# Loads of the inverse transform three ahead instead of five, in place of an output tail cut into column halves

## The chip, the cores and the metric

The kernel runs on one core of one Trainium2 chip. The metric is the device time of one execution in microseconds (us). Engines are named as in the profile: PE is TensorE (PEld its weight loads), DVE VectorE, ACT ScalarE, POOL GpSimd, SP SyncE; SPq, ACTq and POOLq are the queues in which these engines issue DMA transfers.

## The reference

Two computations that share nothing but the output tensor, whose two column halves they fill.

Part A is a recurrent attention block. The 2048 rows of x are taken in 64 segments of 32. Each segment is set behind 8 memory rows; the 40 rows h are projected and attend to each other in 32 heads of 128; the first 8 rows of the result are the next segment's memory. So the segments run one after the other.

```python
mem = mem0
for s in range(64):
    h = concat([mem, x[32 * s:32 * s + 32]])            # 40 x 1024
    q, k, v = h @ Wq, h @ Wk, h @ Wv                    # each 40 x 4096 (32 heads x 128)
    p = softmax(where(mask, q @ k.T / sqrt(128), -1e9)) # mask: a memory row sees all, others no later row
    o = (p @ v) @ Wo                                    # 40 x 1024
    mem, out[s] = o[:8], o[8:]
```

Part B is a long convolution. A kernel K of 2048 taps for each of 1024 channels is the real part of a sum over 128 complex exponentials; y is the convolution of u with K by a transform of length 4096, taken back to time, and out = y + u * Dskip. Only the last step matters here: each piece of the inverse transform needs its piece of u again.

## The kernel before

**Part B runs first, and part A's weights are loaded under its end.** The inverse works through 32 chunks (`todo`, four column quarters of eight). `inverse` (L1316) multiplies on PE (L1313), scales on ACT (L1329), multiplies the chunk of u by Dskip (L1330) and adds (L1331) on DVE, and POOL sends the chunk out (L1332). `load_inverse` (L1270) fetches a chunk of u through SP (L1273) into one of six tiles `uu`. `inverses` (L1286) does one chunk and then issues the load of the chunk NIV - 1 = 4 places further on in what is left, so the loads run NIV = 5 chunks ahead of use. With six tiles, the load of chunk n + 5 takes the tile of chunk n - 1 and waits until that chunk has gone out. SP issues in program order: whatever stands behind such a load waits with it. Behind it stand part A's weights: the generator `residents` issues blocks of 512 KB (L229), a few at a time, from the loop over b and after each of the last eight chunks (ten after the first of them, L1388).

**Part A's loop (`part_a`, L373) goes over 64 segments.** A weight unit is 128 x 2048 bf16 (512 KB). A segment needs 64 units: 8 each for k, q and v in two halves of the heads, and 16 for the output projection (o). 49 stay in SBUF, 3 are held partly in PSUM banks ("kept": k 0 7, q 0 7, o 15) and are copied into SBUF each segment (L292), and 12 are streamed from HBM each segment by SP (L297) into four tiles `wst`, in the order of use; the load of a streamed unit takes the tile of the fourth one before it. `STREAM` and `STREAM_O` name the streamed ones. PE works through the units in order (L381 for q, k and v, L489 for o): the 32 rows are the stationary side, four column strips of PE run at once, and a whole unit takes 0.2165 us from start to start. Between them stand transposes (L392), scores (L406, L410) and value products (L460, L464).

**The seam of two segments.** The eight memory rows of the last projection must be transposed into `hT` (L369) before the next segment's first unit. In the kernel before, the last two output units (13 and 15) are run in column halves, first columns 0 to 127 into `pp`, then columns 128 to 255 into a bank of their own (`po`). ACT copies the first half out (L593) while the second runs; one transposition (`memory(0)`, L368, L369) serves the units of even kc; the other (`memory(1)`) stands after the next segment's first unit, in a part of the bank `pl` that also holds the last value product. The kept unit k 0 7 is copied partly by ACT (L327) and partly by DVE. ACT's copies of `pl` and `pp` into the output tile are L608 and L609. The copy of the second value product `o1` out of PSUM is made in two parts (L477), and the output units are taken in the order 8, 10, 12, 14, 9, 11, so that the first four need its first part alone.

Everything that lives only within a segment stands in one hand-placed block of SBUF (`arena`); `AT` holds the places.

Of the kernel before, what the change touches and what calls it, by code (L numbers as in the profile page):

```python
# [10 lines left out]
BF16 = mybir.dt.bfloat16  # L11
F32 = mybir.dt.float32
I32 = mybir.dt.int32
ALU = mybir.AluOpType
# [7 lines left out]

STREAM = {("k", 0): (2,), ("q", 0): (2,), ("k", 1): (1, 5), ("q", 1): (4,), ("v", 0): (2, 7), ("v", 1): (4, 7)}
STREAM_O = (4, 8, 13)

BANK = {("k", 0): "b0", ("q", 0): "b1", ("k", 1): "b2", ("q", 1): "b0", ("v", 0): "b3", ("v", 1): "b2"}
KEPT = {("k", 0, 7): (("K7a", 0, 512), ("K7b", 512, 512), ("K7c", 1024, 512), ("K7d", 1536, 384), (None, 1920, 128)),
# [3 lines left out]
SLOTS = 4  # L33

ARENA = 5984
AT = {"K7a": 3072, "K7b": 0, "K7c": 4864, "K7d": 4096, "ob": 2048, "pk": 1024, "vx": 4352, "Q7a": 3072, "Q7b": 4960,
      "k0": 0, "q0": 4352, "KT0": 3072, "QT0": 0, "k1": 3072, "q1": 0, "pn0": 2048, "pt0": 5344, "KT1": 3072, "QT1": 0,
      "pb0": 3072, "V0": 2048, "L0": 0, "o0": 3072, "V1": 0, "pn1": 5248, "pt1": 5664, "pb1": 1024, "lb1": 2048,
      "ln1": 2048, "lt1": 2368, "L1": 3072, "o1": 4960, "Oa": 1024, "Ob": 3584}


def weight_blocks(Wq, Wk, Wv, Wo):
# [190 lines left out]
def part_a(ctx, tc, x, src, WD, HE, seg_len, out_a, ahead, W_res, rest, places, first):  # L233
    nc = tc.nc
    S, Dm = x.shape
    M = 8
    SL = seg_len
    E = 128
    KC = Dm // 128
    NS = S // SL  # L240
    assert SL == 32 and M == 8 and Dm == 1024 and HE == 4096
    XM = 24
# [5 lines left out]
    ident, mask, BD, BDx, BDL, hT = ahead.consts  # L248
# [10 lines left out]
    between = {}  # L259

    def unit(key):
        if key in rest:

            rest.remove(key)
            load_resident(tc, wres, src, key, W_res, None, places.pop(0)() if places else None)
        if key in W_res:
            return W_res[key]
        if key in KEPT:
            return ahead_of.pop(key) + halves.get(key, [])
        between.pop(key, lambda: None)()  # L270
        if key in first:
            return first.pop(key)
        return stage(key, WD[key][:])
# [8 lines left out]
    def at(name, *dims):  # L282

        n = int(np.prod(dims))
        t_ = arena[:, AT[name] // 2:AT[name] // 2 + n]
        if len(dims) == 1:
            return t_
        names = "abc"[:len(dims)]
        return t_.rearrange("p (%s) -> p %s" % (" ".join(names), " ".join(names)), **dict(zip(names, dims)))

    def words(out, in_):
        nc.vector.tensor_scalar(out=out.bitcast(I32), in0=in_.bitcast(I32), scalar1=0, scalar2=None, op0=ALU.bitwise_or)  # L292
# [7 lines left out]
    def load_kept(key):  # L300
        t_ = first.pop(key) if key in first else stage(key, src(key))
        kept[key] = {}
        for n in (1,) if key in HALF else (0, 1):
            kept[key][n] = ps_k.tile([128, 512], F32, name="keep", tag="keep%d" % sum(len(b) for b in kept.values()))
            words(kept[key][n][:], t_[:, 1024 * n:1024 * n + 1024])
        if key in HALF:
            t_ = ahead.low["half"] if key[0] == "q" else wres.tile([128, 1024], BF16, name="Whalf")
            nc.sync.dma_start(out=t_[:], in_=src(key)[:, 0, :] if key[0] == "o" else src(key)[:, 0:1024])
            halves[key] = [(0, 1024, t_)]
# [6 lines left out]
            words(t_, kept[key][lo // 1024][:, lo % 1024 // 2:(lo % 1024 + n) // 2])  # L316
            ahead_of[key].append((lo, n, t_))

    def fetch_bits(eng, key, pieces):

        for name, lo, n in pieces:
            t_ = at(name, n) if name else S_[:, 0:n]
            bits = kept[key][lo // 1024][:, lo % 1024 // 2:(lo % 1024 + n) // 2]
            if eng is nc.vector:
                words(t_, bits)
            else:
                eng.copy(out=t_, in_=bits.bitcast(BF16))  # L327
            ahead_of[key].append((lo, n, t_))

    def columns(w, lo, n):  # L330

        if not isinstance(w, list):
            return [(0, w[:, lo:lo + n])]
        return [(max(lo, l_) - lo, t_[:, max(lo, l_) - l_:min(lo + n, l_ + n_) - l_]) for l_, n_, t_ in w if l_ < lo + n and lo < l_ + n_]
# [28 lines left out]
    load_kept(("k", 0, 7))  # L363
    fetch(("k", 0, 7))
    pk = load_pk(0)

    def memory(j):
        nc.tensor.transpose(out=tr_o[j].rearrange("p a b -> p (a b)"), in_=osb[:, 128 * j:128 * j + 128], identity=ident[:])  # L368
        nc.vector.tensor_copy(out=hT[:, :, XM:SL].rearrange("p (q j) r -> p j q r", j=2)[:, j], in_=tr_o[j][:, :, XM:SL])  # L369

    between["q", 0, 2] = lambda: load_kept(("q", 0, 7))
    between["v", 0, 7] = lambda: load_kept(("o", 15))
    for s in range(NS):  # L373
        def quads(m, t, kcs, a=None):
            if a is None:
                a = ps.tile([128, 512], F32, name="acc", tag=BANK[m, t])
            for kc in kcs:
                w = unit((m, t, kc))
                for g in range(4):
                    for o_, rhs in columns(w, 512 * g, 512):  # L380
                        nc.tensor.matmul(a[32 * g:32 * g + 32, o_:o_ + rhs.shape[1]], lhsT=hT[:, kc, :], rhs=rhs,  # L381
                                         start=(kc == 0), stop=(kc == KC - 1), tile_position=(0, 32 * g), skip_group_check=True)
            return a
# [87 lines left out]
            pv(p[:], t, V, pb.rearrange("p a b c -> p a (b c)"), lbs)  # L471
            return p

        def evac_o(p, name, parts=1):
            o, n = at(name, 4, 4, SL), 4 // parts
            for i in range(0, 4, n):
                nc.scalar.copy(out=o[:, i:i + n], in_=p[:, i:i + n, :].rearrange("p a (g q) -> p a g q", g=4))  # L477
            return o

        def pv_l(pl, t, V, L):  # L480

            pv(pl, t, V, L[:, 0].rearrange("p (a b) k -> p a (b k)", a=4), [L[:, 1].rearrange("p a k -> p (a k)")])

        def oblock(po, u, w, oT, lo, n, start=False):
            for hh in range(2):
                h = 2 * u + hh
                for qt in range(4):
                    for o_, rhs in columns(w, 1024 * hh + 256 * qt + lo, n):
                        nc.tensor.matmul(po[32 * qt:32 * qt + 32, o_:o_ + rhs.shape[1]], lhsT=oT[:, h % 4, (h % 16) // 4, :], rhs=rhs,  # L489
                                         start=start and hh == 0, stop=(h == 31), tile_position=(0, 32 * qt), skip_group_check=True)  # L490

        def oproj(po, us, oT):
            for u in us:
                oblock(po, u, unit(("o", u)), oT, 0, 256)

        a = quads("k", 0, (0,))
        if s:
            fetch_bits(nc.vector, ("k", 0, 7), KEPT["k", 0, 7][0:1])
            memory(1)
            fetch_bits(nc.vector, ("k", 0, 7), KEPT["k", 0, 7][1:2])  # L500
        quads("k", 0, (2, 4, 6, 1, 3, 5, 7), a)
        k0 = evac(a, "k0")
        a = quads("q", 0, range(0, 6))
        fetch(("q", 0, 7))
# [10 lines left out]
        vx = load_vx(s)  # L515
# [63 lines left out]
        powers(sc1, 1)  # L579
        oproj(pp[:, 1, :], range(0, 5), o0)  # L580
        pv1 = pv_x(1, V1, pb1, [lb1])
        o1 = evac_o(pv1, "o1", 2)
        lt1 = turn(weigh(sc1, 1, "ln1"), "lt1")
        oproj(pp[:, 1, :], range(5, 8), o0)
        L1 = left_blocks(lt1[:, 0:4, :], lt1[:, 4, :], "L1")
        fetch(("o", 15))
        oproj(pp[:, 1, :], (8, 10, 12, 14, 9, 11), o1)
        ob = at("ob", 2, 256)
        osb, base = ob[:, 0, :], ob[:, 1, :].bitcast(F32)
        ends = [(u, unit(("o", u))) for u in (13, 15)]  # L590
        for u, w in ends:
            oblock(pp[:, 1, 0:128], u, w, o1, 0, 128)
        nc.scalar.copy(out=osb[:, 0:128], in_=pp[:, 1, 0:128])  # L593
        nc.scalar.copy(out=base, in_=pp[:, 1, 128:256])
        rest_o = ps.tile([128, 128], F32, name="po", tag="b2")
        for u, w in ends:
            oblock(rest_o[:], u, w, o1, 128, 128, u == 13)
        last = ps.tile([128, 512], F32, name="pl", tag="b1")
        pv_l(last[:, 0:128].rearrange("p (a k) -> p a k", a=4), 1, V1, L1)
        if s + 1 < NS:  # L600
            tr_o = [ps.tile([128, 4, SL], BF16, name="tro", tag="b0")[:], last[:, 256:320].bitcast(BF16).rearrange("p (a b) -> p a b", a=4)]
            memory(0)
        nc.vector.tensor_tensor(out=osb[:, 128:256], in0=rest_o[:], in1=base, op=ALU.add)
        if s + 1 < NS:
            ahead_of["k", 0, 7] = []
            fetch_bits(nc.scalar, ("k", 0, 7), KEPT["k", 0, 7][2:])
            pk = load_pk(s + 1)
        nc.scalar.copy(out=ob[:, 1, 128:256], in_=last[:, 0:128])  # L608
        nc.scalar.copy(out=ob[:, 1, 0:128], in_=pp[:, 0, 0:128])  # L609
        if s + 1 < NS:  # L610
            stores(s, ob)

# [61 lines left out]
def part_b(ctx, tc, u, A_re, A_im, B_re, B_im, C_re, C_im, log_dt, Dskip, out_b, ahead, copies, residents, first_state):  # L674
# [37 lines left out]
    with tc.tile_pool(name="b_par", bufs=1) as par, tc.tile_pool(name="b_parh", bufs=2) as parh, tc.tile_pool(name="b_mg", bufs=2) as mg, \  # L712
# [54 lines left out]
        def columns(tm):  # L767
            return tm[:].rearrange("p c (k n) -> p c k n", k=4)
# [496 lines left out]
        for j, op in ((0, ALU.add), (1, ALU.subtract)):  # L1265
            v.tensor_tensor(out=Bt[:, kc, j], in0=Y[:, 0], in1=Y[:, 1], op=op)

    NIV = 5

    def load_inverse(dq, c):  # L1270
        r, mc = c // 4, c % 4
        uu = iv.tile([128, 2, DQ], BF16, name="uu", tag="uu", bufs=NIV + 1)
        sy.dma_start(out=uu[:], in_=u_v[r][:, mc:mc + 2, DQ * dq:DQ * dq + DQ])  # L1273
        return uu

# [272 lines left out]
```

## Time and profile before

| what | value |
|---|---|
| times of three runs | 2107.09, 2106.52, 2100.48 us; median 2106.52 |
| the profiled execution | 2107.09 us, its span 2105.4 us |
| busy share of the span | PE 90%, DVE 65%, PEld 57%, ACT 53%, POOL 18% |
| mean granted PE clock | 0.972 |
| first chunk of u loaded | 511.4 us |
| first PE work of part A | 701.56 us |
| first transposition of the memory (end of the first segment) | 759.99 us |
| last one (end of segment 63) | 2020.32 us |

From the last two rows, 62 segments lie between 759.99 and 2020.32 us, 20.33 us each; the shortest usual period is 19.90 us. A row of the timeline gives start, duration, engine, line, operation, output<-input, how many instructions were merged, and in brackets the idle time before and what ended it. A row of the waits gives who waited for whom, us in total, how often, and the longest.

### The profile page before, as it was taken

What the parts mean: (1) busy time and instruction counts of PE and PEld (TensorE: products, weight loads), DVE (VectorE), ACT (ScalarE), POOL (GpSimd) and SP (SyncE); (2) the same over time, 40 slices, a digit from 0 to 9 for tenths busy, and PEclk for the clock granted to TensorE, in tenths of its full rate; (3) what the DMA queues carried; (4) which work ended last, traced back from release to release, by engine and by line L of the source; (5) the groups of instructions that cost most, each with busy time, mean ns of one, the idle gap of its engine ahead of it and who ended that gap; (6) DMA issues with size and microseconds to landing.
All of it is one profiled execution on the core that took longest, in us unless ns stands there. A gap on an engine that the chain in (4) does not pass through costs nothing.

```text
span 2105.4 us, 81063 instructions
## 1 busy us (share of the span) xinstructions
PE 1886.3 (90%) x34694; PEld 1190.3 (57%) x34694; DVE 1368.4 (65%) x3227; ACT 1117.5 (53%) x2170; POOL 388.9 (18%) x780
## 2 busy tenths in 40 slices
PE   2799999978999779999999999999999999999989
PEld 1365665657788435555555555555555555555544
DVE  8689999889898236555565555655556565555650
ACT  5899999951323335445445454454545454454430
POOL 3133433452011101111111111111111111111120
PEclk8799999989999789999999999999999999999999
DMA  7696985665635899999999999999999899999991
GB/s 193 172 252 206 262 238 161 181 190 185 224 131 168 320 341 337 325 333 331 326 335 332 339 331 328 336 337 333 336 328 336 311 336 331 326 334 329 330 348 34
DMA packets 344029, 590.94 MB, mean 281 GB/s; under 512 B 108536, under 2 KB 220184, under 8 KB 341620
## 3 DMA queue, kind: packets, MB, share of 16 engines
q1 hardware_dynamic: 297016, 528.00, 74.3%
q0 software_dynamic: 10544, 33.69, 4.8%
q10 hardware_dynamic: 36108, 24.07, 3.7%
q8 instruction: 272, 4.46, 0.8%
q14 instruction: 89, 0.73, 0.1%
HBM read 530.86 MB, written 65.26 MB: 283 GB/s over the span
## 4 chain that ended last, share of the span: by engine, by line
PE 47%; DMA 19%; ACT 16%; DVE 9%; issue 7%; SPq 2%; POOL 1%; ACTq 0%; DVEq 0%; POOLq 0%
PE acc L381 22%; DMA wst<-WD_v 8%; PE pp L489 8%; DMA wst<-WD_o 6%; PE pe L638 3%; PE tr L392 2%; ACT sn L1142 2%; ACT nr L1151 2%; PE yp L1313 2%; ACT E L1125 2%; PE hps L1087 2%; ACT arena L327 2%; DMA arena<-PKd 1%; PE pa L1117 1%; PE pro L167 1%
## 5 line engine op out<-in xcount | busy, mean ns | idle before, releaser
L381 PEld LDWEIGHTS <-a_hT 128*32 128x32 bf16 x12352 | 339.0, 96 | 335.2 <-issue 82.4
L387 ACT CAST arena<-acc 128x512 bf16<-128x512 f32 x384 | 225.0, 586 | 339.1 <-PE acc L381 315.9
L381 PE MATMUL acc<-W,a_hT 128*32 128x512 bf16 x4864 | 377.2, 383 | 0.3 <-issue 0.3
L489 PEld LDWEIGHTS <-arena 128*32 128x32 bf16 x9216 | 216.1, 97 | 107.9 <-issue 58.4
L381 PE MATMUL acc<-wst,a_hT 128*32 128x512 bf16 x2304 | 233.3, 383 | 21.5 <-DMA wst<-WD_v 15.5
L292 DVE TENSOR_SCALAR arena<-keep 128x256 int32<-128x256 int32 (+1 forms) x386 | 143.4, 399 | 76.1 <-PE acc L381 72.6
L381 PE MATMUL acc<-MF,a_hT 128*32 128x512 bf16 x2048 | 171.3, 383 | 0.0
L489 PE MATMUL pp<-W_o,arena 128*32 128x256 bf16 x4608 | 163.0, 275 | 7.4 <-DMA W_o<-in_A_Wo_dram 7.4
L395 POOL COPY arena<-arena 128x128 bf16<-128x128 bf16 x128 | 37.6, 294 | 707.8 <-PE tr L392 373.9
L426 ACT ACTIVATE sc<-sc 128x160 f32<-128x160 f32 (+1 forms) x192 | 63.9, 333 | 160.9 <-DVE sc L423 157.6
L430 DVE TENSOR_REDUCE a_mx<-sc 128x4 f32<-128x160 f32 (+1 forms) x192 | 73.1, 381 | 87.3 <-ACT sc L426 87.3
L167 PE MATMUL pro<-xTl,wsl 128*128 128x512 bf16 x512 | 121.5, 389 | 8.4 <-ACT xTl L111 5.2
L1087 PEld LDWEIGHTS <-MF 128*128 128x128 bf16 x1024 | 102.2, 100 | 29.2 <-issue 8.6
L422 DVE TENSOR_REDUCE a_mx<-sc 128x4 f32<-128x160 f32 (+1 forms) x192 | 71.6, 373 | 68.6 <-PE sc L410 68.6
L513 DVE COPY arena<-tr 128x512 bf16<-128x512 bf16 x64 | 27.2, 425 | 126.3 <-PE tr L392 126.3
L453 POOL TENSOR_TENSOR arena<-arena,a_BD 128x128 bf16<-128x128 bf16 x128 | 51.6, 403 | 302.0 <-DVE arena L440 198.0
L1313 PE MATMUL yp<-Bt,MI 128*128 128x256 bf16 x680 | 105.5, 277 | 0.8 <-ACT yb L1329 0.8
L1087 PE MATMUL hps<-KT,MF 128*128 128x256 bf16 x720 | 93.3, 281 | 14.0 <-DVE x L1256 11.0
L477 ACT CAST arena<-pv 128x256 bf16<-128x256 f32 (+1 forms) x192 | 79.1, 449 | 47.0 <-PE pp L460 35.3
L1125 ACT ACTIVATE E<-pa 128x648 bf16<-128x648 f32 x128 | 91.4, 714 | 19.0 <-PE pa L1117 11.6
L167 PEld LDWEIGHTS <-wsl 128*128 128x128 bf16 x512 | 50.9, 99 | 73.6 <-issue 21.1
L445 DVE TENSOR_TENSOR arena<-arena,a_BDx 128x512 bf16<-128x512 bf16 x128 | 57.5, 450 | 49.6 <-PE sc L410 47.7
(323 smaller groups left out, 4108.8 us busy)
## 6 DMA issues: line engine op xcount, KB each, us to landing
wst<-WD_v SPq DMA_DIRECT2D x256, 512.0 KB
wst<-WD_k SPq DMA_DIRECT2D x192, 512.0 KB
wst<-WD_o SPq DMA_DIRECT2D x192, 512.0 KB
wst<-WD_q SPq DMA_DIRECT2D x128, 512.0 KB
Ud<-ux POOLq DMA_DIRECT2D x16, 1024.0 KB, 5.0
uq<-Ud SPq DMA_DIRECT2D x32, 512.0 KB
wsl<-in_A_Wk_dram SPq DMA_DIRECT2D x16, 512.0 KB
wsl<-in_A_Wv_dram SPq DMA_DIRECT2D x16, 512.0 KB
```

What stands on the lines that cost most here:

```text
L167: nc.tensor.matmul(a[:], lhsT=w[:, kc, 128 * j:128 * j + 128], rhs=xTl[:, kc, :, :].rearrange("p s k -> p (s k)"), start=(kc == 0), stop=( ...
L292: nc.vector.tensor_scalar(out=out.bitcast(I32), in0=in_.bitcast(I32), scalar1=0, scalar2=None, op0=ALU.bitwise_or)
L381: nc.tensor.matmul(a[32 * g:32 * g + 32, o_:o_ + rhs.shape[1]], lhsT=hT[:, kc, :], rhs=rhs, start=(kc == 0), stop=(kc == KC - 1), tile_pos ...
L387: nc.scalar.copy(out=q, in_=a[:])
L422: nc.vector.tensor_reduce(out=m_, in_=x, axis=AX.X, op=ALU.max)
L426: nc.scalar.activation(out=flat(sc, i), in_=flat(sc, i), func=ACT.Exp, scale=scale)
L430: nc.vector.tensor_reduce(out=m_, in_=x, axis=AX.X, op=ALU.add)
L477: nc.scalar.copy(out=o[:, i:i + n], in_=p[:, i:i + n, :].rearrange("p a (g q) -> p a g q", g=4))
L489: nc.tensor.matmul(po[32 * qt:32 * qt + 32, o_:o_ + rhs.shape[1]], lhsT=oT[:, h % 4, (h % 16) // 4, :], rhs=rhs, start=start and hh == 0, ...
L1087: pe.matmul(s_[r][half][:, cs, :], lhsT=MF[:, kc, 4 * rr + mc, cs, :], rhs=rhs, start=(i == 0 and mc == 0), stop=(i == 1 and mc == 3), ski ...
L1125: sc.activation(out=T["E", r, e // 4][:, lo:lo + 8 * NE].rearrange("p (i c) -> p i c", i=2), in_=T.pop(("p", r, e))[:, :, 0:4 * NE], func= ...
L1313: pe.matmul(yp[:, b, :], lhsT=m_[:, b, cs, kc, :], rhs=Bt[:, kc, j, half, c_, :], start=(kc == 0 and cs == 0 and half == 0), stop=(kc == 3 ...
```

## The change

Two things. `NIV` becomes 3: the load of chunk n + 3 is issued after chunk n, into the same six tiles, so it takes the tile of chunk n - 3. And the seam of part A takes another form: all sixteen output units run whole, in order, into `pp`; then ACT copies both column halves, PE does the last value product into a bank of its own, both transposes and then goes on to the next segment, whose first eight units run without a break; DVE copies both memory parts and then all five pieces of the kept unit k 0 7. `o1` is copied in one piece. With this go another choice of the twelve streamed units, another place in the first segment where two kept units are loaded, and other places in the arena.

```diff
-STREAM = {("k", 0): (2,), ("q", 0): (2,), ("k", 1): (1, 5), ("q", 1): (4,), ("v", 0): (2, 7), ("v", 1): (4, 7)}
-STREAM_O = (4, 8, 13)
+STREAM = {("k", 0): (2, 3), ("q", 0): (4,), ("k", 1): (3,), ("q", 1): (4,), ("v", 0): (0, 6), ("v", 1): (1, 5)}
+STREAM_O = (1, 5, 9)
...
-    between["q", 0, 2] = lambda: load_kept(("q", 0, 7))
-    between["v", 0, 7] = lambda: load_kept(("o", 15))
+    between["q", 0, 4] = lambda: load_kept(("q", 0, 7))
+    between["v", 0, 6] = lambda: load_kept(("o", 15))
...
-        a = quads("k", 0, (0,))
-        if s:
-            fetch_bits(nc.vector, ("k", 0, 7), KEPT["k", 0, 7][0:1])
-            memory(1)
-            fetch_bits(nc.vector, ("k", 0, 7), KEPT["k", 0, 7][1:2])
-        quads("k", 0, (2, 4, 6, 1, 3, 5, 7), a)
+        a = quads("k", 0, (0, 2, 4, 6, 1, 3, 5, 7))
...
-        o1 = evac_o(pv1, "o1", 2)
+        o1 = evac_o(pv1, "o1")
...
-        oproj(pp[:, 1, :], (8, 10, 12, 14, 9, 11), o1)
+        oproj(pp[:, 1, :], range(8, 16), o1)
         ob = at("ob", 2, 256)
-        osb, base = ob[:, 0, :], ob[:, 1, :].bitcast(F32)
-        ends = [(u, unit(("o", u))) for u in (13, 15)]
-        for u, w in ends:
-            oblock(pp[:, 1, 0:128], u, w, o1, 0, 128)
-        nc.scalar.copy(out=osb[:, 0:128], in_=pp[:, 1, 0:128])
-        nc.scalar.copy(out=base, in_=pp[:, 1, 128:256])
-        rest_o = ps.tile([128, 128], F32, name="po", tag="b2")
-        for u, w in ends:
-            oblock(rest_o[:], u, w, o1, 128, 128, u == 13)
-        last = ps.tile([128, 512], F32, name="pl", tag="b1")
-        pv_l(last[:, 0:128].rearrange("p (a k) -> p a k", a=4), 1, V1, L1)
+        osb = ob[:, 0, :]
+        for j in range(2):
+            nc.scalar.copy(out=osb[:, 128 * j:128 * j + 128], in_=pp[:, 1, 128 * j:128 * j + 128])
+        pl = ps.tile([128, 4, 32], F32, name="pl", tag="b2")
+        pv_l(pl[:], 1, V1, L1)
         if s + 1 < NS:
-            tr_o = [ps.tile([128, 4, SL], BF16, name="tro", tag="b0")[:], last[:, 256:320].bitcast(BF16).rearrange("p (a b) -> p a b", a=4)]
-            memory(0)
-        nc.vector.tensor_tensor(out=osb[:, 128:256], in0=rest_o[:], in1=base, op=ALU.add)
+            pt_o = [ps.tile([128, 4, SL], BF16, name="tro", tag=tag) for tag in ("b0", "b1")]
+            for j in range(2):
+                nc.tensor.transpose(out=pt_o[j][:].rearrange("p a b -> p (a b)"), in_=osb[:, 128 * j:128 * j + 128], identity=ident[:])
+            for j in range(2):
+                nc.vector.tensor_copy(out=hT[:, :, XM:SL].rearrange("p (q j) r -> p j q r", j=2)[:, j], in_=pt_o[j][:, :, XM:SL])
         if s + 1 < NS:
-            ahead_of["k", 0, 7] = []
-            fetch_bits(nc.scalar, ("k", 0, 7), KEPT["k", 0, 7][2:])
+            fetch(("k", 0, 7))
+        nc.scalar.copy(out=ob[:, 1, 0:128], in_=pp[:, 0, 0:128])
+        if s + 1 < NS:
             pk = load_pk(s + 1)
-        nc.scalar.copy(out=ob[:, 1, 128:256], in_=last[:, 0:128])
-        nc.scalar.copy(out=ob[:, 1, 0:128], in_=pp[:, 0, 0:128])
+        nc.scalar.copy(out=ob[:, 1, 128:256], in_=pl[:].rearrange("p a k -> p (a k)"))
...
-    NIV = 5
+    NIV = 3
...
-        uu = iv.tile([128, 2, DQ], BF16, name="uu", tag="uu", bufs=NIV + 1)
+        uu = iv.tile([128, 2, DQ], BF16, name="uu", tag="uu", bufs=2 * NIV)
```

`memory`, `oblock` and `fetch_bits` go away with their last callers, and the table `AT` holds other offsets.

## The prediction

> **What bounds the kernel now.** I read the page first, then busy time by stretches, then the SP and POOL timelines where a stretch looked odd, then one seam of the loop row by row, and last the loop's waits.
>
> ```profile
> span 2105.4 us, 81063 instructions
> DMA  7696985665635899999999999999999899999991
> ```
>
> From slice 14 on the transfers are 90% busy, but slices 12 and 13 (579 to 684 us) have 3 and 5 tenths. The stretches (columns: length, busy time and instructions of PE, PEld, DVE, ACT, POOL, then PE clock, DMA share, GB/s):
>
> ```profile
> 660.00:684.70 24.70, 23.46 (x214) 20.64 (x213) 20.77 (x27) 9.33 (x20) 3.03 (x5) 1.00 0.36 116
> 706.00:733.00 27.00, 17.41 (x180) 7.57 (x180) 8.28 (x21) 5.50 (x9) 3.23 (x5) 0.57 0.80 298
> 733.00:760.00 27.00, 14.67 (x258) 7.43 (x256) 6.94 (x23) 4.52 (x12) 2.34 (x6) 0.68 1.01 373
> 760.00:2020.30 1260.30, 1180.63 (x27285) 689.82 (x27281) 725.85 (x2294) 621.56 (x1488) 166.18 (x434) 1.00 0.94 331
> ```
>
> Just ahead of part A the transfers idle (0.36); in its first segment they are the bound (1.01 from 733 to 760, PE busy half the time). The loop after it has PE and the transfers both near full (94% and 0.94). Why they idle is in the SP queue, and in the POOL issues of finished chunks:
>
> ```profile
> 659.60 25.10 SPq L1273 DMA_DIRECT2D uu<-in_B_u_dram  x5
> 684.75 1.41 SPq L229 DMA_DIRECT2D W<-in_A_Wq_dram  x3
> ```
>
> ```profile
> 669.34 0.73 POOL L1332 DMA_DIRECT2D out_dram<-uu  x1 [3.14 <-DVE x L1256]
> ...
> 681.98 0.73 POOL L1332 DMA_DIRECT2D out_dram<-uu  x1 [1.80 <-issue]
> ```
>
> SP spends 25.1 us on five small loads of u, and ten weight blocks stand behind them. Now the seam in a segment without a transfer wait:
>
> ```profile
> 1185.47 0.28 PE L489 MATMUL pp<-wst,arena 128*32 128x128 bf16 x8
> ...
> 1186.18 0.27 ACT L593 CAST arena<-pp 128x128 bf16<-128x128 f32 x1 [1.81 <-PE pp L489]
> 1186.26 0.26 PE L460 MATMUL pl<-arena 128*128 128x32 bf16 x4
> 1186.50 0.23 PE L368 MATMUL tro<-a_ident,arena 128*128 128x128 bf16 x1
> 1186.77 0.17 DVE L369 COPY a_hT<-tro 128x32 bf16<-128x32 bf16 x1 [0.82 <-PE tro L368]
> 1187.00 0.40 PE L381 MATMUL acc<-Wlow,a_hT 128*32 128x512 bf16 x4 [0.27 <-DVE a_hT L369]
> 1187.88 0.22 PE L368 MATMUL pl<-a_ident,arena 128*128 128x128 bf16 x1 [0.48 <-ACT arena L608]
> 1188.02 0.40 PE L381 MATMUL acc<-wst,a_hT 128*32 128x512 bf16 x4
> ```
>
> From the first half block (1185.47) to the second unit of the next segment (1188.02) PE takes 2.55 us, and it stops twice: for DVE's copy of the memory, and for ACT's L608, which reads the bank that the second transposition writes. The loop's waits say that both come in nearly every segment, and what the transfers cost beside them:
>
> ```profile
> PE pl L368 <- ACT arena L608: 27.9, 59, 0.6
> PE acc L381 <- DVE a_hT L369: 16.5, 62, 0.3
> PE acc L381 <- DMA wst<-WD_v: 13.9, 24, 1.3
> PE pp L489 <- DMA wst<-WD_o: 6.4, 14, 0.9
> ```
>
> **Part 1, loads of u three ahead.** The same loads, each later in SP's order by two chunks, with a tile that came free two chunks earlier. The ten weight blocks stand behind one such load. Before it is that of chunk 29, in the tile of chunk 23, whose store POOL issues at 681.98; the store's issue ends at 682.71 and the load starts at 684.33, so 1.6 us later. After, it is that of chunk 27, in the tile of chunk 21: issued at 669.34, ended 670.07, so the load starts near 671.7 and the blocks near 672.1 instead of 684.75: 12.7 us earlier. Nothing else holds the first six (they wait for earlier transfers alone); the seventh needs a chunk's product that ends at 672.1. What they then run into: the last loads of u now queue behind the ten blocks (some 14 us at 1.4 us each), and DVE waits in order for them; but in the kernel before it waits there too (8.7 us, until 704.5), and PE starts part A at 701.56 only. So the gain is that of the backlog of the first segment, which ends with its last weights at 760. It is bounded below by the loads that wait for DVE's copy of the first kept unit (705.84; it can move to about 702): 4 us. Above: the 12.7 us, and half of the 5.4 us that the transfers idle in 706 to 733 (27 x 0.2), which makes 15. I take 12, near the shift itself, because the stretch that ends last, 733 to 760, is at 1.01.
>
> The Trainium skill ("TensorE: Matmul & The Clock Gate", Part 1) has the PE clock halved after a window of some 3.4 us without work and restored after as long a busy one. The rows have 0.57 and 0.68 in the first segment, after a stop of 5.08 us at 707.04. By that rule the earlier blocks would also keep the clock up, and the first stretch would give up to 5 us more; since transfers end the segment, I count none of it.
>
> **Part 2, the seam on PE.** Removed: the two units in halves, both stops, L594's copy, L603's addition. Added, from the first of the last two units: two whole units, 2 x 0.2165 = 0.43, and 0.03 for one more piece of the kept one; the last matmul ends 0.17 after its strip could go on (0.27 long, 0.109 apart at 256 columns); ACT starts 0.06 later; from ACT's start to the first unit takes 1187.00 - 1186.18 = 0.82, the value product and both transposes lying within it; one unit 0.22 to the second. Sum 1.73 instead of 2.55: -0.82. Against it, `o1` comes in one copy of 0.586 us instead of a first part of 0.378, and PE waits for it already: +0.21. Net -0.61 per segment, from 19.90 to 19.3.
>
> A new wait could come from the kept unit k 0 7, now five DVE copies behind both memory copies. Counted from the start of DVE's first memory copy (1186.77), it begins them at 0.18 (two steps of 0.09, as the next DVE row at 1186.86 shows) and ends the last at 0.18 + 3 x 0.333 + 0.265 + 0.209 = 1.65 (steps from copy to copy as such rows have them); PE starts its first unit at 0.23 and reaches the kept one seven units, 1.52 us, later, at 1.75. It fits with a tenth to spare: bounds 0 and +0.3. PE's end is thus -0.3 to -0.8, and I take -0.6. Queued behind these copies on DVE is nothing until the next scores; ACT, freed of three copies, issues the next pk load no later.
>
> **Part 3, the streamed units.** Still twelve, and the same bytes: 12 x 524288 + 131072 + 114688 + 2 x 65536 = 6.67 MB per segment. At the loop's 331 GB/s that is 20.1 us, at the 373 of the first segment's end 17.9. So a PE period of 19.3 is possible, but with less idle between transfers. By the skill's 436 GB/s ("DMA: Bandwidth & Descriptors", Bandwidth) it would be 15.3 us, the transfers would not matter, and the seam's 0.61 would be had whole, 38 us; no stretch here comes near that rate.
>
> Their places matter more. A load begins when the fourth streamed unit before it has been used, so the time between these two uses is what it has. From the PE rows this was 6.0 to 7.7 us for all twelve. With the new places, counted in units of 0.2165 us and the blocks between, it is 4.5 (v 1 5), 5.6, 5.1 and 5.2 (o 1, 5, 9), 5.8 (v 1 1), 6.7 to 7.0 for three and 7.1 to 8.3 for the last four. The chain has such loads at 5.4 to 7.5 us under load. The long leads empty the queue ahead of the short ones, so these find it freer, but the cover is thin: PE would wait there for anything from nothing to 0.9 us more than the 0.43 per segment by which the mean of 20.33 stands over 19.90. I take 0.45, half way, about what a lead of 5.1 us lacks against a load of 5.5. Net per segment -0.61 + 0.45 = -0.16, over 62 to 63 segments -10 us.
>
> **Sum.** The profiled execution took 2107.09 us (1.7 over its span, 0.6 over the median of the three). 2107.1 - 12 - 10 = 2085.
>
> **Rivals.** (a) The transfers keep up and the seam shows whole: -12 - 38 gives 2057. For it: 373 GB/s was reached, and loop segments without any wait exist. Against: mean share 0.94 and 5.1 us leads. (b) Slower: the four short leads (v 1 5 and o 1, 5, 9) starve PE. If their loads take 6.5 us, v 1 5 alone comes 2 us late, and a part of it, say 1.1 us, recurs in every segment: +0.5 x 63 - 12 = +19, so 2126. It decides from 0.80 us of additional wait per segment (0.61 plus 12/63); then the gain of part 1 is gone. (c) Three ahead does not do what it says, because the weights are held by something else (DVE's copy, PE's release of tiles): -3 instead of -12, so 2094 with the loop as forecast, and about 2104 if the loop gains nothing.
>
> **How the numbers follow.** The forecast (a gain of both parts, 2070 to 2100) has 0.68, (a) 0.10, (b) 0.10, (c) 0.12. The range reaches from 2064, part of (a) and the seam's upper bound with little wait, to 2104, (c) with an idle loop; what is left out is the far half of (a), and (b). A measurement of this kernel can tell about 0.3%, 6.3 us, from no change. Faster by more: the forecast, (a) and half of (c), 0.84. Within: half of (c) and the mild end of (b), 0.08. Slower: the rest of (b), 0.08.
>
> **What would show it.** Right: the ten W loads issue near 672, and the first transposition of a memory comes near 748; the stretch 660 to 685 has a DMA share over 0.7; no wait on L608's kind; shortest loop period 19.1 to 19.4 and the mean near 20.2; waits on WD_v and WD_o that grow from 20 us to 45 or more. Wrong: a first segment that still ends near 760; a wait of the k 0 7 unit for DVE in every segment; a mean period over 20.6, with waits at v 1 5.

## The result, and the profile after

The changed kernel is slower: 2120.66 us (median of 22 runs, 2108.85 to 2135.74) against 2113.53 us for the kernel before (22 runs, 2100.48 to 2119.38), ratio 1.0039 with a 95% interval of 1.0022 to 1.0056. The forecast was 2085, with a range that ended at 2104. The profiled execution took 2122.74 us, 2 over its median; the one shown of before (2107.09) was 6 under the median of its 22 runs. So of the 15.6 us between the two spans, about half belongs to which execution was drawn.

Counted from the first chunk of u loaded, the first segment ends at 250.1 us (763.85 - 513.76), before at 248.6 (759.99 - 511.43). From there to the last transposition of a memory, 62 segments take 20.57 us each, before 20.33. Both parts of the forecast's gain are missing: the 12 us of the first segment, and the loop, which became 0.24 us per segment longer instead of 0.16 shorter.

The busy time by stretches, as it was shown of before (after each engine's busy time: clock, DMA share, GB/s):

```profile
660.00:684.70 24.70, 24.09 (x221) 21.44 (x220) 22.43 (x26) 8.99 (x17) 2.92 (x4) 1.00 0.70 219
...
706.00:733.00 27.00, 10.58 (x129) 5.00 (x123) 6.29 (x15) 3.30 (x7) 4.69 (x7) 0.66 0.57 190
733.00:760.00 27.00, 16.26 (x252) 7.33 (x245) 9.04 (x28) 6.85 (x13) 2.71 (x6) 0.69 1.00 359
760.00:2039.00 1279.00, 1182.04 (x26388) 683.83 (x26379) 776.03 (x2418) 549.65 (x1241) 184.33 (x434) 1.00 0.94 327
```

The idle transfers did not go, they moved: 660 to 685 rose from 0.36 to 0.70 as forecast, but 706 to 733 fell from 0.80 to 0.57. The SP queue shows the first half of this, and POOL's queue the second; the last row is SP's wait for these stores in 700 to 735 us (us in total, how often, the longest):

```profile
662.85 13.21 SPq L1245 DMA_DIRECT2D uu<-in_B_u_dram  x5
676.11 1.41 SPq L229 DMA_DIRECT2D W<-in_A_Wq_dram  x3
...
732.41 0.33 SPq L308 DMA_DIRECT2D Whalf<-in_A_Wo_dram  x1
```

```profile
694.63 0.73 POOL L1304 DMA_DIRECT2D out_dram<-uu  x1 [5.04 <-issue]
701.06 0.73 POOL L1304 DMA_DIRECT2D out_dram<-uu  x1 [5.70 <-issue]
706.60 0.73 POOL L1304 DMA_DIRECT2D out_dram<-uu  x1 [4.81 <-issue]
...
730.05 0.73 POOL L1304 DMA_DIRECT2D out_dram<-uu  x1 [1.81 <-issue]
730.78 0.30 POOL L379 COPY arena<-arena 128x128 bf16<-128x128 bf16 x1
```

```profile
SPq L308 <- DMA out_dram<-uu: 14.7, 3, 7.1
```

The ten weight blocks start at 676.11 instead of 684.75, so SP was freed: counted from the first load of u, 11.0 us earlier (forecast 12.7). But `Whalf`, the half unit of o 15, is loaded at 732.41 only, 2.36 us after POOL issued the last chunk's store (730.05); before it was 728.37 after 726.01, the same 2.36. It lies in space that the stores free: SP waits for them at L308, for 14.7 us, where before it came there later and waited 5.6. All late weights of o stand behind it on SP. POOL sends its stores 5.5 to 6.4 us apart in the first rows shown, and the last one 19 us after DVE finished that chunk (710.8). The first segment ends 31.4 us after `Whalf` (before 31.6).

A seam without a transfer wait (PE rows, then ACT's first two and DVE's copy), and the loop's waits of PE:

```profile
822.97 0.30 PE L474 MATMUL pp<-Whalf,arena 128*32 128x256 bf16 x4
...
823.51 0.27 ACT L567 CAST arena<-pp 128x128 bf16<-128x128 f32 x1 [2.24 <-PE pp L474]
823.64 0.33 ACTq L327 DMA_DIRECT2D arena<-PKd  x1
823.83 0.40 PE L573 MATMUL tro<-a_ident,arena 128*128 128x128 bf16 x2 [0.19 <-ACT arena L567]
824.10 0.35 DVE L575 COPY a_hT<-tro 128x32 bf16<-128x32 bf16 x2 [1.19 <-PE tro L573]
824.33 0.40 PE L365 MATMUL acc<-Wlow,a_hT 128*32 128x512 bf16 x4
824.55 0.39 PE L365 MATMUL acc<-wst,a_hT 128*32 128x512 bf16 x4
```

```profile
PE acc L365 <- DMA wst<-WD_v: 32.0, 52, 1.9
PE pp L474 <- DMA wst<-WD_o: 16.5, 31, 1.7
PE tro L573 <- ACT arena L567: 11.2, 58, 0.2
PE tr L376 <- ACT arena L371: 7.5, 11, 1.5
PE sc L390 <- DVE arena L489: 5.3, 8, 0.9
```

The seam is what was forecast. Unit 15 starts at 822.97 and unit 14 0.2165 earlier, so from there to the second unit of the next segment it is 1.80 us (forecast 1.73, before 2.55), with 0.82 from ACT's start to the first unit. Both old stops are gone. Waits for WD_v and WD_o are 48.5 us, as forecast (45 or more). The forecast has nothing for the last two rows (PE waits for ACT's copy of k 1 and for `KT0`), nor for what stands behind them on ACT and DVE:

```profile
ACT arena L371 <- DMA out_dram<-arena: 45.4, 20, 4.4
...
DVE arena L489 <- DMA OLd<-arena: 27.7, 10, 3.5
```

These are waits for the stores of the output tile `ob` (in the kernel before ACT waited once, for 3.8 us). ACT's row for the other store, OLd (21.4 us, 10 times), is left out: the third kernel below has 41.0 us of it although `ob` there shares no byte with what these copies write, so the name says nothing of the cause. One segment of 21.82 us, ACT's rows:

```profile
844.60 0.33 ACTq L327 DMA_DIRECT2D arena<-PKd  x1
...
846.10 0.57 ACTq L347 DMA_DIRECT2D out_dram<-arena  x1
...
854.40 0.33 ACTq L333 DMA_DIRECT2D arena<-VXd  x1
854.82 0.59 ACT L371 CAST arena<-acc 128x512 bf16<-128x512 f32 x1 [3.99 <-DMA out_dram<-arena]
855.30 0.43 ACT L410 ACTIVATE sc<-sc 128x320 f32<-128x320 f32 x1
```

and the chain of that stretch has `846.10 8.28 DMA out_dram<-arena` as its longest piece. ACT issues the load of `vx` (L333) in its own order. In the changed table `vx` (bytes 3392 to 4288) shares bytes with `ob` (3904 to 4928), so this issue waits until the store of `ob` has landed, 8.28 us after its issue, and with it waits what ACT has next: the copy of k 1 and the exponentials. By the trace, the landing of that store released this load in 58 of 62 segments, 4.7 to 9.0 us after the store's issue; in the traces of the kernel before and of the third kernel below it did so in none. `KT0` (4704 to 5984, DVE and POOL) and `q1` (4288 to 5312, ACT) lie on `ob` too. In the table before, `ob` (2048 to 3072) meets none of the three; the first to take its bytes is `pn0`, later still.

### The profile page after: what moved, and what is told of

Read it like the earlier page. It is cut to its first block, busy times and chain, and to the rows that moved or that the text cites. A ratio compares the mean times of both kernels' runs of the same rounds, so it can differ in the third digit from the quotient of the medians.

```text
span 2121.0 us, 78639 instructions
## 1 busy us (share of the span) xinstructions
PE 1877.8 (89%) x33734; PEld 1179.9 (56%) x33734; DVE 1418.4 (67%) x3352; ACT 1044.2 (49%) x1917; POOL 411.1 (19%) x780
## 4 chain that ended last, share of the span: by engine, by line
PE 36%; DMA 23%; DVE 2%; ACT 2%; issue 1%; ACTq 1%; SPq 0%; DVEq 0%
PE acc L365 20%; DMA wst<-WD_v 10%; PE pp L474 9%; DMA wst<-WD_o 7%; PE pe L610 3%; DMA out_dram<-arena 2%; DMA OLd<-arena 2%; PE tr L376 2%; DMA W_o<-in_A_Wo_dram 1%; PE pv L444 1%; DMA wst<-WD_q 1%; PE sc L390 1%; PE pv L448 1%; ACT arena L567 1%; PE tro L573 1%
## 5 line engine op out<-in xcount | busy, mean ns | idle before, releaser
L365 PEld LDWEIGHTS <-a_hT 128*32 128x32 bf16 x12352 | 334.7, 96 | 329.3 <-issue 76.5
L474 PEld LDWEIGHTS <-arena 128*32 128x32 bf16 x8256 | 211.1, 97 | 112.0 <-issue 56.7
L292 DVE TENSOR_SCALAR arena<-keep 128x256 int32<-128x256 int32 (+1 forms) x512 | 175.8, 394 | 34.7 <-PE acc L365 30.9
L474 PE MATMUL pp<-W_o,arena 128*32 128x256 bf16 x4608 | 171.0, 275 | 10.8 <-DMA W_o<-in_A_Wo_dram 7.2
L365 PE MATMUL acc<-MF,a_hT 128*32 128x512 bf16 x2048 | 158.7, 382 | 0.0
L460 ACT CAST arena<-pv 128x512 bf16<-128x512 f32 x128 | 75.2, 587 | 86.7 <-PE pp L444 66.1
L437 POOL TENSOR_TENSOR arena<-arena,a_BD 128x128 bf16<-128x128 bf16 x128 | 71.2, 556 | 224.1 <-DVE arena L424 211.3
L567 ACT CAST arena<-pp 128x128 bf16<-128x128 f32 x128 | 27.8, 269 | 164.8 <-PE pp L474 164.8
L1097 ACT ACTIVATE E<-pa 128x648 bf16<-128x648 f32 x128 | 91.4, 714 | 18.4 <-PE pa L1089 12.8
L575 DVE COPY a_hT<-tro 128x32 bf16<-128x32 bf16 x126 | 21.5, 175 | 111.4 <-PE tro L573 111.4
```

The costliest lines, as they stand in the source:

```text
L437: nc.gpsimd.tensor_tensor(out=L[:, 0].rearrange("p (a b) k -> p a b k", a=4), in0=bc(lt[:, :, 0:XL].unsqueeze(2), [128, 4, 4, XL]), in1=bc ...
L460: nc.scalar.copy(out=o, in_=p[:].rearrange("p a (g q) -> p a g q", g=4))
L1097: sc.activation(out=T["E", r, e // 4][:, lo:lo + 8 * NE].rearrange("p (i c) -> p i c", i=2), in_=T.pop(("p", r, e))[:, :, 0:4 * NE], func= ...
```

## The experiments

Theory: (i) three loads ahead gain nothing, since POOL's last chunk store sets the end of the first segment; (ii) the seam is worth what was forecast; (iii) the new places of the streamed units cost something, and (iv) the new arena places, which the forecast did not price, turn the stores of `ob` into a wait. Rivals: the transfers' rate alone sets the loop, or the loads of u lost the time. Periods and first segments (from the first load of u) come from one profiled execution each, times from 4 to 28 runs. Kernels with the same loop show how far a period can be trusted: 20.33, 20.39 and 20.42 for the loop of before (before, 1, 12), 20.57 and 20.68 for the changed one (after, 2), 20.12 and 20.20 (3, 7), 20.01, 19.90 and 19.91 (6, 8, 9). The experiments ran in three groups (1 to 4, 5 to 8, 9 to 12), each beside the kernel before; across groups, ratios to it are compared, and not times. A table of all stands at the end.

**1. Three ahead, alone.** On the kernel before:

```diff
-    NIV = 5
+    NIV = 3
...
-        uu = iv.tile([128, 2, DQ], BF16, name="uu", tag="uu", bufs=NIV + 1)
+        uu = iv.tile([128, 2, DQ], BF16, name="uu", tag="uu", bufs=2 * NIV)
```

> The kernel before with the loads of u three ahead and nothing else changed. Theory: the first segment ends about 34 us after POOL has sent the last chunk out (before: 726.01 and 759.99, after: 730.05 and 763.85), because the half unit of o 15 is loaded into space that this store frees, and all late weights of o stand behind it on SP. The earlier weight blocks only fill the transfers earlier, so that more of POOL's stores are sent at the 5.7 us pace of 698 to 726 instead of the 3 us pace of 669 to 682. So the ten blocks start near 673 to 676, the last store comes at 726 to 731, the first transposition of a memory at 760 to 765, the loop keeps its 20.33 us, and the time is 0 to 5 us over the kernel before. Rival (the prediction's part 1): the first segment ends near 748 and the time falls by 12 us.

Measured 2112.09 against 2110.92 us, ratio 1.0004 (0.9979 to 1.0030); period 20.39. `Whalf` again follows the last store by 2.36 us:

```profile
720.39 0.73 POOL L1332 DMA_DIRECT2D out_dram<-uu  x1 [1.81 <-issue]
```

```profile
722.75 0.33 SPq L308 DMA_DIRECT2D Whalf<-in_A_Wo_dram  x1
```

In this execution the segment ended at 752.73, earlier than expected (243.1 after the first load of u), 30.0 after `Whalf`; over the runs nothing of it is left. The 12 us (0.57%) lie outside the interval.

**2. Five ahead in the changed kernel.** The same edit backwards.

> The changed kernel with the loads of u five ahead again (and NIV + 1 tiles, which is six as before). Theory: the first segment ends near 760 to 762, as in the kernel before, the loop keeps the 20.57 us per segment of the changed kernel, so the whole loss of the change lies in the loop, and the time is 0 to 4 us under the changed kernel. Rival: the loads of u are where the 8 us were lost, and the time falls to that of the kernel before.

2122.41 us, ratio to before 1.0045 (1.0017 to 1.0072), where the changed kernel has 1.0039. Period 20.68, first segment 245.3 (last store 723.15, `Whalf` 725.50). The depth of these loads neither made the loss nor hides a gain, within some 7 us.

**3. `ob` apart.** The changed kernel with another table `AT`, of which this matters:

```diff
-AT = {... "ob": 3904, ... "vx": 3392, ... "KT0": 4704, ... "q1": 4288, ...}
+AT = {... "ob": 3936, ... "vx": 3040, ... "KT0": 1344, ... "q1": 4960, ...}
```

> The changed kernel with another table of arena places and nothing else: the output tile ob shares no byte with KT0, vx and q1, which in the changed kernel are written 4.5 to 9 us after ob's stores are issued, while such a store takes 4 to 8.3 us to land; the first to take ob's bytes is now pt0, later still. Theory: the waits of ACT and DVE for the stores of ob (45 + 21 us on ACT, 28 us on DVE in the changed kernel) go, with them PE's waits for ACT's copies of k1 and for KT0; PE's waits for streamed weights take a part of it back since the transfers are busy 0.94 of the loop. Segment 20.57 to 20.2 us, time 15 to 25 us under the changed kernel. Rival (transfers alone set the loop): the waits for weights take all of it back, segment 20.5 or more, time within 6 us of the changed kernel.

2094.16 us, ratio to before 0.9931 (0.9910 to 0.9951): 1.1% under the changed kernel's ratio, some 23 us, and now faster than the kernel before. Period 20.12 instead of 20.57. PE's two rows for k 1 and KT0 (12.8 us) are gone, ACT's for out_dram is down to one of 3.4 us, and the waits for streamed weights did not take them back, they fell too, from 51.5 to 39.1 us. Together that is 25 of the 28 us by which the 62 segments became shorter:

```profile
PE acc L365 <- DMA wst<-WD_v: 29.5, 70, 1.7
PE tro L573 <- ACT arena L567: 12.0, 59, 0.5
PE pp L474 <- DMA wst<-WD_o: 8.0, 17, 1.2
```

```profile
ACT arena L371 <- DMA out_dram<-arena: 3.4, 1, 3.4
```

Theory (iv) holds. The table was laid out anew as a whole, so which of the three neighbours of `ob` costs how much stays open.

**4. Eleven streamed units**, in the changed kernel:

```diff
+        key = ("v", 1, 4) if key == ("v", 1, 5) else key
```

With this, v 1 5 leaves the streamed units, and its weights are left out of the result.

> The changed kernel with eleven streamed units instead of twelve: the place of v 1 5 is taken by the resident weights of v 1 4, so that part of the products is computed from other weights, at the same work on PE. It takes away 524288 of 6.67 million bytes per segment, 7.9%, and the shortest lead (4.5 us). Theory A (the transfers set the mean period): the period falls by about a twelfth of 20.57, to 19.0 to 19.3, time 80 to 100 us lower. Theory B (the short lead of v 1 5 alone was at fault, the transfers have room): it falls only by the waits for that unit, to 20.1 to 20.3. Theory C (the waits for the stores set it): hardly any change.

2077.78 us, ratio 0.9848 (0.9814 to 0.9881), period 19.99. 7.9% fewer bytes gave 2.8% of the period: a little more than theory B, far less than A, and none of the three alone. The stores' waits are still there (34.8 us on ACT for out_dram).

**5. The changed kernel's streamed units in the kernel before.**

```diff
-STREAM = {("k", 0): (2,), ("q", 0): (2,), ("k", 1): (1, 5), ("q", 1): (4,), ("v", 0): (2, 7), ("v", 1): (4, 7)}
-STREAM_O = (4, 8, 13)
+STREAM = {("k", 0): (2, 3), ("q", 0): (4,), ("k", 1): (3,), ("q", 1): (4,), ("v", 0): (0, 6), ("v", 1): (1, 5)}
+STREAM_O = (1, 5, 9)
```

The places in the first segment where two kept units are loaded go with it, as in the change.

> The kernel before with the streamed units of the changed kernel, its seam and its arena as they were. By the order of PE's work the shortest lead (time from the use of the fourth streamed unit before to the use of this one) is then 4.5 to 5 us at v 1 5, 5.0 to 5.8 at the three o units, instead of 5.2 to 7.2 for all. Theory: short leads cost more than long ones give back: PE's waits for streamed weights grow from 20.7 us in the loop to 45 or more, segment 20.33 to 20.6 or 20.7, time 15 to 25 us over the kernel before. Rival (only the mean load of the transfers counts, not the places): segment 20.3 to 20.4, time the same.

2120.14 us, ratio 1.0022 (1.0009 to 1.0035), period 20.59. The wait is where it was forecast, at the v units (13.9 us before); those of o did not grow:

```profile
PE acc L381 <- DMA wst<-WD_v: 27.8, 62, 1.7
...
PE pp L489 <- DMA wst<-WD_o: 5.1, 9, 1.2
```

Theory (iii) holds, at a lower price than expected (15 to 25 us): 0.17 to 0.27 us per segment against the three traces of the loop of before, about 0.1 by the medians (5.4 us over 62).

**6. `ob` apart and the streamed units of before.** The third kernel with the edit of the fifth backwards.

> The changed kernel with ob apart (as in the third run) and the streamed units of the kernel before, at even leads. Theory: the waits at v 1 5 shrink (29.5 us for the v units in the third run to 10 to 15), segment 20.12 to 19.8 to 19.95, time 10 to 20 us under the third run. Rival (the transfers' own rate sets what is left: 0.95 busy at 334 GB/s): PE's waits only move to other units, segment 20.05 to 20.15, time within 5 us of the third run.

2085.01 us, ratio 0.9855 (0.9831 to 0.9878), period 20.01, a little more than expected; by the ratios 16 us under the third kernel. Waits at the v units fell from 29.5 to 7.3 us:

```profile
PE pp L474 <- DMA wst<-WD_o: 11.1, 19, 1.1
PE pp L474 <- ACT arena L460: 9.5, 36, 0.3
PE acc L365 <- DMA wst<-WD_v: 7.3, 13, 0.8
```

This kernel is the new seam with the two other loop edits taken out. Its shortest usual period is 19.30 us (five segments have it), the figure that the forecast worked out for the seam; the mean moved by less, 0.32 here and 0.4 in the two other kernels with this loop (8, 9). What takes the rest is shown in part only: PE's waits for weights are 23.7 us against 20.7 before, and those for the copy of `o1` 9.5 against 0.6.

**7. The last eight chunk stores through ACT**, on the third kernel:

```diff
-        gp.dma_start(out=out_v[r][:, mc:mc + 2, d], in_=uu[:])
+        (sc if dq == 3 else gp).dma_start(out=out_v[r][:, mc:mc + 2, d], in_=uu[:])
```

> The changed kernel with ob apart (third run), and the stores of the last eight chunks issued in ACT's queue instead of POOL's. Theory: the first segment is held by the last chunk store, since the half unit of o 15 is loaded into space that this store frees (first transposition of a memory 32.3 to 34.0 us after POOL's last store in five traces, wherever that store stood between 720 and 730). ACT's issues take 0.4 us and do not wait for an earlier store, so the last one comes 1 to 3 us after DVE's last addition, near 705 to 712 instead of 722, and the first transposition at 740 to 748 instead of 756: time 8 to 15 us under the third run. Rival: the late weights of o are held by the transfers alone (0.99 to 1.01 busy in 733 to 760) and the end of the first segment stays within 3 us.

2079.66 us, ratio 0.9839 (0.9811 to 0.9868), by the ratios some 19 us under the third kernel. Last store, `Whalf`, and the stretch that had been half idle:

```profile
699.49 0.38 ACTq L1304 DMA_DIRECT2D out_dram<-uu  x1
```

```profile
705.94 0.34 SPq L308 DMA_DIRECT2D Whalf<-in_A_Wo_dram  x1
```

```profile
706.00:733.00 27.00, 17.61 (x316) 8.40 (x316) 10.73 (x32) 8.83 (x16) 2.96 (x7) 0.81 1.04 390
```

The first segment ends at 739.61, 231.9 us after the first load of u (third kernel 245.6). SP no longer waits for a store at L308: `Whalf` is issued 0.55 us after the load before it. So POOL's stores did hold it.

**8. All three.** `ob` apart, even streamed units, ACT stores.

> All three together on the changed kernel: ob apart, the streamed units of the kernel before, and the last eight chunk stores in ACT's queue. If the three are independent, the gains of the third, sixth and seventh run add up: 17 us under the kernel before by the third, 10 to 20 more by the places, 8 to 15 more by the stores, so 2060 to 2075 us, 1.7 to 2.4% under the kernel before. Rival: places and stores give nothing, and it stands where the third run stood, 2090 to 2097.

2068.39 us, ratio 0.9778 (0.9751 to 0.9806): the gains roughly add up (50 us by the ratios of 3, 6 and 7, measured 46), and with the eleventh this is the best version that computes the whole reference: 2.2% under the kernel before. Period 19.90, first segment 239.3. In the same group, ACT's queue for the stores is worth 16.6 us (from 6 to 8) and the even places 11.3 (from 7 to 8).

**9. The eighth kernel with five loads ahead** (`NIV` 5, six tiles).

> The kernel of the eighth run with the loads of u five ahead again: with POOL's stores out of the way, this asks what part 1 of the change is worth by itself. Theory (the prediction's part 1, with its cover taken away): the ten weight blocks start 8 to 12 us later, and since the end of the first segment is now set by the transfers, it comes 4 to 12 us later after the first load of u than in the eighth run (239.3 us; in the seventh 231.9), time 2072 to 2080 against 2068. Rival (the transfers catch up before the segment ends): within 3 us of the eighth run.

2074.42 us, ratio 0.9821 (0.9789 to 0.9853); first segment 241.1. The interval overlaps that of the eighth kernel. What three ahead is worth once POOL is out of the way is between nothing and some 18 us (the ratios differ by 0.0043, and 0.0028 and 0.0032 are their half widths), and stays open. The traces show how it shrinks: five ahead, the ten blocks start 8.4 us later than in the eighth kernel, `Whalf` 3.2 and the end of the segment 1.7.

**10. `ob` apart and eleven streamed units**, the edits of 3 and 4.

> The third run (ob apart) with eleven streamed units, v 1 5 being computed from the resident weights of v 1 4. With the stores' waits gone and 7.9% of the bytes taken away, this tells what rate the transfers allow. If they set what is left of the mean (0.95 busy at 334 GB/s), the period falls by 6 to 8%, to 18.9 (PE's own work without a wait, by adding up the usual shortest stretches of a segment) to 19.1. If the places and single late loads set it, it falls by the waits for v 1 5 alone, to 19.4 to 19.6. Time 2030 to 2055.

2060.81 us, ratio 0.9752 (0.9726 to 0.9777), period 19.72: above both expectations. Against the third kernel, 7.9% fewer bytes gave 2.0%, while the transfers ran slower:

```profile
760.00:1980.00 1220.00, 1168.49 (x26334) 674.62 (x26330) 781.95 (x2415) 552.54 (x1240) 173.34 (x434) 1.00 0.92 315
```

They moved 334 GB/s at 0.95 in the third kernel. So a rate of the transfers is not what sets the loop. PE's shortest period is 19.29 here, and single waits stand on top of it: the rows have 17.7 us for late weights and 12.4 for the copy of `o1`, from 765 to 2000 us.

**11. The copy of `o1` in two parts**, on the eighth kernel:

```diff
-        o1 = evac_o(pv1, "o1")
+        o1 = evac_o(pv1, "o1", 2)
-        oproj(pp[:, 1, :], range(8, 16), o1)
+        oproj(pp[:, 1, :], (8, 10, 12, 14, 9, 11, 13, 15), o1)
```

> The kernel of the eighth run with the copy of o1 in two parts, as in the kernel before, and the output units in the order 8, 10, 12, 14, 9, 11, 13, 15, of which the first four need the first part alone. PE waits 10.4 us in the loop for the copy in one piece (38 times, 0.3 at most), which PE's first matmul then no longer does. If PE sets a part of the period, segment 19.90 to 19.75 to 19.85, time 3 to 9 us lower; if the transfers set it, the time stays within 3 us of 2068.

2069.61 us, ratio 0.9775 (0.9742 to 0.9809), period 19.90: no difference, though the intervals leave room for some 9 us either way. Its shortest periods are 19.21 to 19.23 instead of 19.30, so the copy in one piece costs 0.08 where nothing else waits (the forecast had 0.21). PE's 10 us of waits for this copy went, and came back as waits for weights (19.7 to 29.0 us, for k, q, v and o together).

**12. ACT stores in the kernel before**, the edit of 7 alone.

> The kernel before with the stores of the last eight chunks issued in ACT's queue, and nothing else. Theory: the last of them comes some 8 to 14 us earlier than POOL's (726 in the profile of before), the first segment ends 5 to 14 us earlier counted from the first load of u (248.6 us before), the loop keeps 20.33, time 2100 to 2109 against 2114 of the kernel before in the last call. Rival: without the loads of u three ahead, the weights behind them start as late as ever and nothing is had.

2108.48 against 2114.72 us, ratio 0.9970 (0.9953 to 0.9987): 6 us. Last store 709.61, first segment 243.8 instead of 248.6. The gain is had without the loads three ahead.

**All of them side by side.** The four columns in the middle are us after the first load of u: the start of the ten weight blocks, the last chunk store, `Whalf`, the end of the first segment.

| kernel | loads ahead | last stores by | ten blocks | last store | `Whalf` | end | period | ratio |
|---|---|---|---|---|---|---|---|---|
| before | 5 | POOL | 173.3 | 214.6 | 216.9 | 248.6 | 20.33 | 1 |
| 5 | 5 | POOL | 172.2 | 212.5 | 214.8 | 245.0 | 20.59 | 1.0022 |
| 2 | 5 | POOL | 171.9 | 211.8 | 214.1 | 245.3 | 20.68 | 1.0045 |
| after | 3 | POOL | 162.4 | 216.3 | 218.6 | 250.1 | 20.57 | 1.0039 |
| 1 | 3 | POOL | 158.3 | 210.8 | 213.1 | 243.1 | 20.39 | 1.0004 |
| 3 | 3 | POOL | 159.2 | 211.6 | 214.0 | 245.6 | 20.12 | 0.9931 |
| 4 | 3 | POOL | 158.9 | 213.0 | 215.3 | 244.4 | 19.99 | 0.9848 |
| 6 | 3 | POOL | 158.6 | 210.6 | 212.9 | 244.9 | 20.01 | 0.9855 |
| 10 | 3 | POOL | 162.0 | 213.8 | 216.1 | 245.4 | 19.72 | 0.9752 |
| 12 | 5 | ACT | 173.2 | 200.0 | 211.6 | 243.8 | 20.42 | 0.9970 |
| 9 | 5 | ACT | 170.4 | 197.1 | 209.0 | 241.1 | 19.91 | 0.9821 |
| 7 | 3 | ACT | 157.2 | 191.7 | 198.2 | 231.9 | 20.20 | 0.9839 |
| 8 | 3 | ACT | 162.0 | 197.1 | 205.8 | 239.3 | 19.90 | 0.9778 |
| 11 | 3 | ACT | 161.4 | 195.7 | 204.3 | 237.7 | 19.90 | 0.9775 |

With POOL's stores, three ahead starts the blocks 10 to 15 us earlier, and the last store, `Whalf` and the end come when they came (`Whalf` 214 to 217 with five, 213 to 219 with three). In every row the end follows `Whalf` by 29 to 34 us.

## Why the prediction was wrong

**Part 1 (-12 us) failed at one sentence: "the stretch that ends last, 733 to 760, is at 1.01", from which it took the shift of the ten blocks as the shift of the end.** That stretch is full, but what fills it cannot start before `Whalf`, and `Whalf` cannot start before POOL's last store has landed. The third rival had the right shape, with the wrong holder: it named DVE's copy and PE's release of tiles. The rows were on the table, since the prediction shows POOL's stores at 669.34 and 681.98; read on to 726.01, the same queue shows steps of 4.4 to 6.2 us between the last six, and `Whalf` 2.36 us behind. The earlier blocks also bring the slow step earlier: POOL's last run of stores that take over 5 us to land begins 168.9 us after the first load of u, before 178.3. SP reached `Whalf` 7.4 us earlier after the first load of u than before, and waited there 9.1 us longer. The forecast's own sign of an error, "a first segment that still ends near 760", came true. In the Trainium skill, "DMA: Bandwidth & Descriptors", the section "SWDGE vs HWDGE vs iDMA" would have pointed at the queue: it sends plain transfers to SP or ACT, and keeps GpSimd for those that cast, accumulate or are irregular. The runs agree: the same eight stores in ACT's queue took 0.38 us each instead of 0.73, and 6 us (12th kernel against before) or 16.6 us (8th against 6th) off the time.

**Part 2 (-0.61 per segment) was right for the shortest period.** 1.80 us for the forecast 1.73, a copy of k 0 7 that is in time (no wait of PE for it in the loop), and a usual shortest period of 19.30 in the sixth kernel. Of the mean period it gave 0.3 to 0.4. The trace of the changed kernel hardly shows it (shortest period 19.49, usually more), because of the next point.

**A term was missing: the arena.** The diff has a new table of arena places, and the sum holds nothing for it. It is the largest of the losses: 20.57 to 20.12, 0.45 us per segment, 28 us in the loop, 23 by the ratios. The prediction said of ACT that it "issues the next pk load no later", which is true; the issue behind it, of `vx`, is the one that waits. A shared byte is a wait like any other, and the question that the prediction put to DVE's queue, what stands behind it, was not put to ACT's: the copy of k 1 and the exponentials.

**Part 3 (+0.45) was oversized.** The mechanism was right, at v 1 5 and its neighbours: the leads came out as counted, 4.6 us at v 1 5 and 5.2 to 5.6 at the o units in the segment that ends at 824 us. They cost 0.1 to 0.27 with the old seam (5th kernel). With the new one they cost 0.11 to 0.30 by the traces (3 against 6, 7 against 8) and 11 to 16 us in time. The short leads of the three o units cost nothing in the fifth kernel (5.1 us for o). The prediction set the new leads beside too long a figure for the old ones: its 6.0 to 7.7 run from start of use to start of use, and from the end of use, as the new ones are counted, the same rows give 5.6 to 7.2. That the waits for WD_v and WD_o reached the forecast 45 or more is partly luck: of the 48.5 us, 37.5 are left when `ob` is apart. And "no stretch here comes near that rate" is too strong: from 688 to 706 us the kernel before moved 353 to 415 GB/s.

In time, by the ratios of kernels 6, 3 and after: three ahead and seam -31 us (forecast -12 - 38), places +16 (forecast +28), arena +23 (forecast nothing), which makes the +8 that was measured. The three steps lead from before to after one by one, so they must add up; each is known to 5 to 7 us. The second rival was right in its sign, and its 2126 is near the measured time by luck: its mechanism, four starving leads, is not what decided. Without the arena term (kernels 3 and 7) the loop would have gained 0.13 to 0.21 per segment, about the 0.16 of the forecast.

## What to carry to other kernels

Where tiles are placed by hand in one block, a new table of places is an edit like any other: list who writes next on the bytes of each tile that a DMA reads, and compare the time between with the landing time of that DMA under load, here 4.7 to 9.0 us. A DMA issue on a compute engine's queue that has to wait stops that engine's arithmetic behind it (3.99 us in the segment shown). Before a transfer is moved earlier, find what the last transfer of the stretch waits for, and look for a store in another queue that frees its space.

## What was not expected of the hardware

POOL's stores of 128 KB are issued at the pace at which they land. In the changed kernel, from 620 to 670 us and then from 688 to 722, where the transfers are busier (share 0.69 and 0.86; columns: KB, median us from issue to landing):

```profile
out_dram<-uu POOLq DMA_DIRECT2D x7, 128.0 KB, 3.8
```

```profile
out_dram<-uu POOLq DMA_DIRECT2D x6, 128.0 KB, 5.6
```

and the issues stand 5.5 to 7.9 us apart in that stretch while chunks are waiting: the store of 694.63 landed after 6.12 us and the next was issued 6.43 after it, that of 712.63 after 7.58 with the next 7.89 after it. Each follows the landing of the one before by 0.3 us. In ACT's queue two of the same stores were issued 1.8 us apart (674.45 and 676.28, 7th kernel). The program gives POOL's descriptors 512 bytes (`SCRATCH`); whether that is the reason was not tried.
